# Transposing the queries and keys of the later chunks on the DMA crossbar instead of TensorE

## The chip, the cores and the metric

The kernel runs on one core of one Trainium2 chip. The metric is the device time of one execution in microseconds; a kernel's time is the median of its runs. A profiled execution has its own span, 1.7 to 2.0 us shorter than the time of the same run.

## The reference

A retention layer (attention with a decay in place of the softmax) over 8 batches, 8 heads, 576 positions and head size 64 makes a matrix of 4608 rows by 512, and a two-layer network with a swish gate runs on those rows:

```python
scores = scale * np.matmul(q, k.transpose(0, 1, 3, 2))
gamma = 1.0 - 2.0 ** (-5.0 - np.arange(H, dtype=np.float32))
Dmat = np.where(rel >= 0, gamma[:, None, None] ** rel[None, :, :], 0.0)
attn = np.matmul(scores * Dmat[None], v)
x = attn.transpose(0, 2, 1, 3).reshape(B * S, H * D)      # 4608 x 512
h = x @ w_in                                             # 512 -> 2048
g = h * (1.0 / (1.0 + np.exp(-beta * h)))
out = g @ w_out                                          # 2048 -> 512
```

## The kernel before

The retention part works in 40 chunks, five a batch: four of 128 positions and one of 64. For each chunk GpSimd casts queries, keys and values to bf16 (`pre`), TensorE transposes queries and keys in eight 128x128 blocks into PSUM and ScalarE copies them to SBUF (`a_T`), TensorE makes the scores (`a_sc`), the running state (`a_st`) and the output (`a_O`). The network works in nine blocks of 512 rows, each with 16 up steps and 16 down steps of four matmuls. The steps of the chunks for the next block are woven between the steps of the present block, at positions counted in fill steps (one fill step is one up or down step, four matmuls); the order in which they are called is the order in each engine's list.

```python
    def pre(i):
        # ...
        qn = sb.tile([P, H, D], BF16, name="qn", tag="qn", bufs=3)
        kn = sb.tile([P, H, D], BF16, name="kn", tag="kn", bufs=3)
        vp = vpads[i % NV]                    # NV = 3 padded value tiles, used in turn
        # ... casts: queries, keys, values (GpSimd from chunk 4 on)

    def a_T(i):
        # ...
        T = psum.tile([P, 2, HP, P], BF16, name="T", tag="T", bufs=1)
        for j, src in enumerate((L["qn"], L["kn"])):
            for p in range(HP):
                nc.tensor.transpose(T[:, j, p, :cL],
                                    src[:cL, 2 * p:2 * p + 2, :].rearrange("p h d -> p (h d)"),
                                    ident[:cL, :cL])
        qkT = sb.tile([P, 2, HP, P], BF16, name="qkT", tag="qkT", bufs=3)
        nc.scalar.copy(qkT[:, :, :, :cL], T[:, :, :, :cL])

    def up(m, fo, t0=0, tn=MB):
        # ...
        ph = psum.tile([P, MB], F32, name="ph", tag="mm", bufs=3)
        for ko in range(KO):
            nc.tensor.matmul(ph[:, :tn], w_in_sb[:, ko, fo * P:(fo + 1) * P], xT[:, ko, x0:x0 + tn], ...)
        nc.scalar.activation(gT[:, fo, t0:t0 + tn], ph[:, :tn], ACT.Silu, scale=beta_sb[:, fo:fo + 1])

    def attn_steps(i, at, gap=2.0):
        return [(at - 4, F(pre, i)), (at - 3.9, F(load_next, i)), (at, F(a_T, i)), (at + gap, F(a_sc, i)),
                (at + 2 * gap, F(a_st, i)), (at + 2 * gap, F(a_O, i))]
```

SyncE issues all loads and stores. Each load of a chunk is three DMAs (queries, keys, values) and runs seven chunks ahead.

## Time and profile before

| | before |
|---|---|
| time, median | 338.75 us (338.43 to 338.87) |
| TensorE busy | 97% of the span |
| ScalarE, VectorE, GpSimd busy | 48%, 34%, 34% |
| granted TensorE clock | 0.994 |

In a group of the profile, the columns are line, engine, operation, output<-inputs, count, then busy us and the mean of one in ns, then the idle time of the engine before them and what ended it. In a timeline they are start us, length us, engine, line, operation, count, and in brackets an idle time and what ended it. Matmul ends are modelled and overlap the next one, so a length in microseconds is read from start to start. The lines of the kernel before stand in the prediction below.

A ruler for what follows: the time from the first up step of block 2 to the first up step of block 8, read from the timeline. In these six blocks all 26 changed chunks are handled and TensorE is the bound. For the kernel before it is 305.50 - 95.89 = **209.61 us**.

### The profile page before, as it was taken

What the parts mean: (1) busy time and instruction counts of PE and PEld (TensorE: products, weight loads), DVE (VectorE), ACT (ScalarE), POOL (GpSimd) and SP (SyncE); (2) the same over time, 40 slices, a digit from 0 to 9 for tenths busy, and PEclk for the clock granted to TensorE, in tenths of its full rate; (3) what the DMA queues carried; (4) which work ended last, traced back from release to release, by engine and by line L of the source; (5) the groups of instructions that cost most, each with busy time, mean ns of one, the idle gap of its engine ahead of it and who ended that gap; (6) DMA issues with size and microseconds to landing.
All of it is one profiled execution on the core that took longest, in us unless ns stands there. A gap on an engine that the chain in (4) does not pass through costs nothing.

```text
span 337.1 us, 6009 instructions
## 1 busy us (share of the span) xinstructions
PE 325.6 (97%) x2455; PEld 174.0 (52%) x2455; DVE 114.0 (34%) x202; ACT 163.1 (48%) x272; POOL 115.0 (34%) x132
## 2 busy tenths in 40 slices
PE   5979899999999999999999999999999999999995
PEld 2644574676554555545555555545555555544442
DVE  4664373623321244213332432223224432320011
ACT  2767671385246623752376227712782257404800
POOL 5224767875324433323334432233333330000000
PEclk9799999999999999999999999999999999999999
DMA  9999999999999737906492549036400100011011
GB/s 173 222 387 212 243 377 214 199 212 229 234 222 246 146 111 172 172 0 158 116 228 48 117 118 214 9 87 159 114 2 31 61 36 0 14 55 57 2 61 63
DMA packets 121979, 46.53 MB, mean 138 GB/s; under 512 B 113232, under 2 KB 113248, under 8 KB 121952
## 3 DMA queue, kind: packets, MB, share of 16 engines
q1 hardware_dynamic: 121920, 46.15, 61.3%
q8 instruction: 19, 0.31, 0.4%
q14 instruction: 8, 0.07, 0.1%
q10 hardware_dynamic: 32, 0.01, 0.0%
HBM read 36.71 MB, written 9.44 MB: 137 GB/s over the span
## 4 chain that ended last, share of the span: by engine, by line
PE 84%; DMA 7%; SPq 4%; issue 1%; DVE 1%; ACT 1%; POOL 0%; POOLq 0%
PE po L285 38%; PE ph L273 32%; DMA qkvn<-in_q_dram 4%; PE O L238 4%; PE T L201 4%; SPq L63 4%; PE sc L217 3%; DMA wt<-in_moe_w_out_dram 2%; PE st L255 2%; PE O L233 2%; SPq L122 1%; ACT gT L275 1%; DVE w_out_sb L141 0%; DVE R L221 0%; ACT qkT L205 0%
## 5 line engine op out<-in xcount | busy, mean ns | idle before, releaser
L273 PE MATMUL ph<-xT,w_in_sb 128*128 128x512 bf16 (+2 forms) x640 | 134.2, 358 | 1.7 <-DVE xT L242 1.7
L285 PE MATMUL po<-w_out_sb,gT 128*128 128x512 bf16 x576 | 133.6, 380 | 0.0
L275 ACT ACTIVATE gT<-ph,beta_sb 128x512 bf16<-128x512 f32 (+2 forms) x160 | 102.0, 645 | 41.2 <-PE ph L273 39.9
L273 PEld LDWEIGHTS <-w_in_sb 128*128 128x128 bf16 x640 | 58.4, 98 | 55.5 <-issue 1.6
L285 PEld LDWEIGHTS <-gT 128*128 128x128 bf16 x576 | 53.3, 98 | 57.9
L221 DVE TENSOR_TENSOR R<-sc,causal 128x512 bf16<-128x512 f32 (+1 forms) x80 | 47.2, 631 | 101.1 <-PE sc L217 101.0
L205 ACT COPY qkT<-T 128x1024 bf16<-128x1024 bf16 (+1 forms) x40 | 36.9, 924 | 68.6 <-PE T L201 68.5
L181 POOL TENSOR_TENSOR qn<-qkvn,gq 128x512 bf16<-128x512 f32 (+1 forms) x36 | 37.9, 1052 | 49.9 <-PE T L201 46.4
L186 POOL TENSOR_TENSOR vpad<-qkvn,gv 128x512 bf16<-128x512 f32 (+1 forms) x40 | 41.6, 1041 | 28.2 <-PE O L238 14.9
L291 DVE COPY ot<-po 128x512 f32<-128x512 f32 x36 | 24.8, 691 | 67.5 <-PE po L285 65.1
L185 POOL CAST kn<-qkvn 128x512 bf16<-128x512 f32 (+1 forms) x36 | 21.9, 608 | 69.5 <-issue 65.7
L261 ACT CAST sbd<-st 64x256 bf16<-64x256 f32 x64 | 23.3, 364 | 43.4 <-PE st L255 42.6
L242 DVE CAST xT<-O 128x512 bf16<-128x512 f32 (+1 forms) x40 | 25.5, 637 | 38.0 <-PE O L238 38.0
L238 PE MATMUL O<-R,vpad 128*128 128x128 bf16 (+1 forms) x320 | 23.7, 214 | 1.4 <-DVE R L221 1.2
L238 PEld LDWEIGHTS <-vpad 128*128 128x128 bf16 (+1 forms) x320 | 18.2, 97 | 2.8 <-issue 2.2
L217 PEld LDWEIGHTS <-qkT 64*128 64x128 bf16 (+1 forms) x320 | 8.9, 98 | 17.3 <-ACT qkT L205 7.1
L201 PE MATMUL T<-ident,qn 128*128 128x128 bf16 (+1 forms) x160 | 15.1, 218 | 2.5 <-DVE qn L181 2.4
L201 PEld LDWEIGHTS <-qn 128*128 128x128 bf16 (+1 forms) x160 | 11.1, 99 | 11.9 <-DVE qn L181 2.4
L217 PE MATMUL sc<-qkT 64*128 64x128 bf16 (+1 forms) x320 | 15.5, 217 | 0.6 <-ACT qkT L205 0.4
L201 PE MATMUL T<-ident,kn 128*128 128x128 bf16 (+1 forms) x160 | 14.9, 216 | 0.3 <-POOL kn L185 0.3
L255 PEld LDWEIGHTS <-kn 128*128 128x128 bf16 x128 | 9.5, 99 | 6.6 <-issue 0.2
L255 PE MATMUL st<-vpad,kn 128*128 128x128 bf16 x128 | 12.7, 222 | 0.0
(40 smaller groups left out, 80.0 us busy)
## 6 DMA issues: line engine op xcount, KB each, us to landing
out_dram<-ot SPq DMA_DIRECT2D x36, 256.0 KB, 2.2
qkvn<-in_q_dram SPq DMA_DIRECT2D x32, 256.0 KB, 4.8
qkvn<-in_k_dram SPq DMA_DIRECT2D x32, 256.0 KB, 5.1
qkvn<-in_v_dram SPq DMA_DIRECT2D x32, 256.0 KB, 5.0
wt<-in_moe_w_in_dram SPq DMA_DIRECT2D x4, 1024.0 KB, 10.6
wt<-in_moe_w_out_dram SPq DMA_DIRECT2D x4, 1024.0 KB, 10.2
qkvn<-in_q_dram SPq DMA_DIRECT2D x8, 128.0 KB, 4.0
qkvn<-in_k_dram SPq DMA_DIRECT2D x8, 128.0 KB, 3.6
```

The lines of the kernel that those rows point to most:

```text
L181: (nc.vector if first else nc.gpsimd).tensor_tensor(qn[:cL], t[:cL, 0], gq_b, ALU.mult)
L186: nc.gpsimd.tensor_tensor(vp4[:cL], t[:cL, 2].rearrange("p (pr two) d -> p pr two d", two=2), gv_b.rearrange("p (pr two) d -> p pr two d", ...
L201: nc.tensor.transpose(T[:, j, p, :cL], src[:cL, 2 * p:2 * p + 2, :].rearrange("p h d -> p (h d)"), ident[:cL, :cL])
L205: nc.scalar.copy(qkT[:, :, :, :cL], T[:, :, :, :cL])
L217: nc.tensor.matmul(sc[j][:cL, p, :cL], L["kT"][r, p, :cL], L["qT"][r, p, :cL], start=True, stop=True, skip_group_check=True)
L221: nc.vector.tensor_tensor(R[:cL, j, :, :cL], sc[j][:cL, :, :cL], m_b, ALU.mult)
L238: nc.tensor.matmul(O[:, p, :cL], vp[:cL, 2 * p + j, :], R[:cL, j, p, :cL], start=(n == 0), stop=(j == 1), skip_group_check=True)
L242: nc.vector.tensor_copy(xT[:, :, n0:n0 + cL], O[:, :, :cL])
L255: nc.tensor.matmul(st[:, p, :], L["kn"][:cL, 2 * p:2 * p + 2, :].rearrange("p h d -> p (h d)"), L["vp4"][:cL, p], start=(c == 0 and p == 0 ...
L273: nc.tensor.matmul(ph[:, :tn], w_in_sb[:, ko, fo * P:(fo + 1) * P], xT[:, ko, x0:x0 + tn], start=(ko == 0), stop=(ko == KO - 1))
L275: nc.scalar.activation(gT[:, fo, t0:t0 + tn], ph[:, :tn], ACT.Silu, scale=beta_sb[:, fo:fo + 1])
L285: nc.tensor.matmul(po[:], gT[:, fo, ms * P:(ms + 1) * P], w_out_sb[:, fo, :], start=(fo == 0), stop=(fo == FO - 1))
```

## The change

Intent: take the transposes off TensorE, which is the bound, and give them to the DMA crossbar (the DMA engines' own transpose, issued with `dma_start_transpose`), for chunks from the last one of batch 2 on (chunk 14), where the loads are less dense. Queries and keys share one tile so that one DMA moves both; buffers grow from three to four; casts and transposes are placed earlier. The whole diff:

```diff
--- before.py
+++ after.py
@@ -64,6 +64,7 @@
         qkv_tiles[(b, c)] = t
 
     NQ = 7
+    XB = 14
     order = [(b, c) for b in range(B) for c in range(NC)]
     for b, c in order[:4]:
         load_chunk(b, c)
@@ -171,8 +172,8 @@
         c0, cL = chunks[c]
         t = qkv_tiles.pop((b, c))
         first = i < 4
-        qn = sb.tile([P, H, D], BF16, name="qn", tag="qn", bufs=3)
-        kn = sb.tile([P, H, D], BF16, name="kn", tag="kn", bufs=3)
+        qk = sb.tile([P, 2, H, D], BF16, name="qk", tag="qk", bufs=4)
+        qn, kn = qk[:, 0], qk[:, 1]
         vp = vpads[i % NV]
 
         vp4 = vp.rearrange("p (pr two) (x d) -> p pr (two x) d", two=2, x=2)[:, :, 0::3, :]
@@ -185,11 +186,21 @@
             nc.gpsimd.tensor_copy(kn[:cL], t[:cL, 1])
         nc.gpsimd.tensor_tensor(vp4[:cL], t[:cL, 2].rearrange("p (pr two) d -> p pr two d", two=2),
                                 gv_b.rearrange("p (pr two) d -> p pr two d", two=2), ALU.mult)
-        live[i] = dict(qn=qn, kn=kn, vp=vp, vp4=vp4)
+        live[i] = dict(qk=qk, qn=qn, kn=kn, vp=vp, vp4=vp4)
 
     def load_next(i):
         if i + NQ < len(order):
             load_chunk(*order[i + NQ])
+
+    def a_X(i):
+
+        b, c = order[i]
+        cL = chunks[c][1]
+        L = live[i]
+        qkT = sb.tile([P, 2, HP, P], BF16, name="qkT", tag="qkT", bufs=4)
+        nc.scalar.dma_start_transpose(qkT.rearrange("p j pr s -> p (j pr) s")[:, :, :cL],
+                                      L["qk"][:cL].rearrange("p j h d -> p (j h d)"))
+        L["qT"], L["kT"] = qkT[:, 0], qkT[:, 1]
 
     def a_T(i):
         b, c = order[i]
@@ -201,7 +212,7 @@
                 nc.tensor.transpose(T[:, j, p, :cL],
                                     src[:cL, 2 * p:2 * p + 2, :].rearrange("p h d -> p (h d)"),
                                     ident[:cL, :cL])
-        qkT = sb.tile([P, 2, HP, P], BF16, name="qkT", tag="qkT", bufs=3)
+        qkT = sb.tile([P, 2, HP, P], BF16, name="qkT", tag="qkT", bufs=4)
         nc.scalar.copy(qkT[:, :, :, :cL], T[:, :, :, :cL])
         L["qT"], L["kT"] = qkT[:, 0], qkT[:, 1]
 
@@ -308,7 +319,10 @@
 
     def attn_steps(i, at, gap=2.0):
 
-        return [(at - 4, F(pre, i)), (at - 3.9, F(load_next, i)), (at, F(a_T, i)), (at + gap, F(a_sc, i)),
+        if i < XB:
+            return [(at - 4, F(pre, i)), (at - 3.9, F(load_next, i)), (at, F(a_T, i)), (at + gap, F(a_sc, i)),
+                    (at + 2 * gap, F(a_st, i)), (at + 2 * gap, F(a_O, i))]
+        return [(at - 10, F(pre, i)), (at - 9.9, F(load_next, i)), (at - 5, F(a_X, i)), (at + gap, F(a_sc, i)),
                 (at + 2 * gap, F(a_st, i)), (at + 2 * gap, F(a_O, i))]
 
     warm_up(12)
```

## The prediction

> **What bounds the kernel now.** I read the busy table first, then the groups, then the chain of work that ended last, then the timeline of one block of rows. The busy table and two of the groups (columns of a group: line, engine, operation, output<-inputs, count | busy us, mean ns of one | idle us before it):
>
> ```profile
> PE 325.6 (97%) x2455; PEld 174.0 (52%) x2455; DVE 114.0 (34%) x202; ACT 163.1 (48%) x272; POOL 115.0 (34%) x132
> ...
> L205 ACT COPY qkT<-T 128x1024 bf16<-128x1024 bf16 (+1 forms) x40 | 36.9, 924 | 68.6 <-PE T L201 68.5
> ...
> L201 PE MATMUL T<-ident,qn 128*128 128x128 bf16 (+1 forms) x160 | 15.1, 218 | 2.5 <-DVE qn L181 2.4
> ...
> L201 PE MATMUL T<-ident,kn 128*128 128x128 bf16 (+1 forms) x160 | 14.9, 216 | 0.3 <-POOL kn L185 0.3
> ```
>
> TensorE is the bound; no other engine passes half of the span. The transposes look like 15.1 + 14.9 = 30 us, but a matmul's end is modelled and overlaps the next one's, so this sum must not be used as a saving. The timeline of TensorE (start us, length, engine, line, operation, count) gives start to start:
>
> ```profile
> 170.62 2.75 PE L273 MATMUL ph<-xT,w_in_sb 128*128 128x512 bf16 x12
> 173.21 0.39 PE L201 MATMUL T<-ident,qn 128*128 128x128 bf16 x4
> 173.43 0.39 PE L201 MATMUL T<-ident,kn 128*128 128x128 bf16 x4
> 173.65 1.89 PE L273 MATMUL ph<-xT,w_in_sb 128*128 128x512 bf16 x8
> 175.48 0.40 PE L217 MATMUL sc<-qkT 64*128 64x128 bf16 x8
> 175.81 1.90 PE L273 MATMUL ph<-xT,w_in_sb 128*128 128x512 bf16 x8
> 177.54 0.39 PE L255 MATMUL st<-vpad,kn 128*128 128x128 bf16 x4
> 177.77 0.39 PE L233 MATMUL O<-qkT,sbd 128*128 128x128 bf16 x4
> 177.99 0.61 PE L238 MATMUL O<-R,vpad 128*128 128x128 bf16 x8
> 178.44 1.89 PE L273 MATMUL ph<-xT,w_in_sb 128*128 128x512 bf16 x8
> 180.26 0.29 PE L201 MATMUL T<-ident,qn 64*128 64x64 bf16 x4
> 180.39 0.28 PE L201 MATMUL T<-ident,kn 64*128 64x64 bf16 x4
> 180.60 1.90 PE L273 MATMUL ph<-xT,w_in_sb 128*128 128x512 bf16 x8
> ```
>
> The reader is to see that TensorE never waits: 12 matmuls of 512 columns take 173.21 - 170.62 = 2.59 us (0.216 each), and everything else is packed against them. Eight transposes of a full chunk take 173.65 - 173.21 = 0.44 us, not 0.8. The 64-row chunk at 180.26 takes 0.34 us plus 0.09 us before it (178.44 + 8 x 0.216 = 180.17). In the window from 100 to 300 us the table by windows has TensorE at 100% of every stretch, granted clock 1.00. So each microsecond of work taken off TensorE there is a microsecond off the span, unless a wait appears.
>
> **What the Trainium skill says.** (1) "VectorE: DVE Perf Modes", section "The three transpose paths", puts a 128x128 bf16 transpose at 390 ns on TensorE and 1309 ns on the crossbar. The trace has 190 to 315 ns for one TensorE transpose and 0.44/8 = 55 ns in a row, so here the TensorE side is seven times cheaper than the page's figure; that caps what the change can win. (2) "Advanced Engine Details and Errata", section "X-Bar Transpose (TRN2)", says that such transposes run about as fast as regular DMAs. No run yet shows it. (3) "DMA: Bandwidth & Descriptors", section "Issuing engines are not separate DMA queues": DMAs of all issuers share 16 engines, and issuing from ScalarE only saves issue time. The trace agrees in so far as the loads, all from SyncE, already fill those engines: DMA share 0.61 from 130 to 170 us, 0.72 to 210, 0.36 to 250, then 0.09. (4) The same page, section "Queues, rings and completion order", gives older generations 262,144 sequencer cycles for 8,192 tiles of an SBUF to SBUF transpose, which is 32 a tile. No row of the trace shows such an issue.
>
> **The change part by part.** Chunks 14 to 39 change, 26 of 40; six of them (the last of batches 2 to 7) have 64 rows.
>
> *Removed from TensorE:* 20 full sets x 0.44 us = 8.8, and 6 short sets x 0.43 = 2.6, together **11.4 us**, all of it in the stretch where TensorE sets the end. The built program agrees: 208 transposes (26 x 8) are gone from its list. If nothing else happened: 338.75 - 11.4 = **327.3 us**.
>
> *Removed from ScalarE:* 20 copies of 1.01 us and 6 of 0.58 = 23.7 us. ScalarE is not the bound, so this is worth nothing by itself.
>
> *Added to ScalarE:* 26 DMA issues. The built program cuts the source into tiles of 16 rows by 128 columns: 8 x 8 = 64 for a full chunk. With 32 cycles a tile and the 1.2 GHz sequencer of "Advanced Engine Details and Errata" (Clock Domains), my estimate is 64 x 32 / 1.2 = 1.7 us of held ScalarE, half of that for a short chunk; the loads' own issues on SyncE took 0.38 to 2.87 us for the queries (median 0.77), so a full queue can stretch it. While ScalarE issues, it evicts no ph. Is that seen? The up-projection makes one ph per 4 x 0.216 = 0.863 us, ScalarE takes 0.69 us for each, and three buffers stand between. Taking the issue that falls at 168.0 us in the trace above: ScalarE is free at 168.45, holds to 170.15, evicts the two waiting tiles by 171.6; TensorE, which has scores, state and output of the earlier chunk to do meanwhile, asks for these buffers at 171.5 and 172.35, and the first was free by 170.9. So 1.7 us hides; past some 2.3 us the excess shows in TensorE. About half of the issues fall into up-projections, the rest into down-projections, where ScalarE has almost nothing to do. I charge 1 us in all.
>
> *Added to the DMA engines:* 26 transfers, 256 KB each for a full chunk. Loads of the same size (1024 packets of 256 bytes) land in 4.8 to 5.1 us in the median, three being issued together; the q1 queue spends 0.613 x 337 x 16 / 121,920 = 27 ns a packet, so 64 packets an engine are 1.7 us of work. Estimate for one transpose: 1.7 us of issue, overlapping 1.7 us of moving, doubled when a load shares the engines, and the 1 to 2 us of tail that the 2.2 us landing of the output stores suggests: 4 to 6 us.
>
> *Moved:* the transpose is issued 5 fill steps before the place of the old one, and scores follow 2 steps after that place. For the chunk transposed at 173.21, five steps before is 167.99 and its scores are at 175.48: 7.5 us, less the 0.44 us that goes, less the 0.45 us until ScalarE is free: 6.6 us. The data arrive in time by 0.6 to 2.6 us if the estimate holds. Inputs are ready: GpSimd's casts move six steps earlier, GpSimd is 34% busy and took 1.04 + 0.61 + 1.04 us a chunk, and the four buffers of queries and keys let it run ahead. I charge 2 us in all for transposes that land late, mainly before 210 us where loads fill the queues.
>
> *Sum:* 338.75 - 11.4 + 1 + 2 = 330.35, rounded to **330 us** (-2.6%).
>
> **The rivals.** *A: the score matmuls wait for late transposes.* For it: the new load of a chunk is issued about when a neighbour's transpose is, on the same engines, with landings up to 14.9 us for one load, and the skill's 1309 ns for one 128x128 block would make eight 10.5 us if they ran one after another. Against it: 6.6 us of lead, and a lead of five steps with four buffers looks chosen with care. If each came 1 us late, 26 us would come back and the time would be some 353 us; a wait in a third of them gives 336.
> *B: ScalarE becomes the bound of the up-projection.* An up-projection needs 16 x 0.72 us of eviction, about 2.5 x 0.74 of state copies and 2.5 issues: 13.4 us + 2.5 issues, against 16 x 0.863 + 2.5 x 1.33 = 17.1 us of TensorE. At 1.7 us an issue this is 17.6 against 17.1, just balanced by the buffers; at 3 us it is 20.9 and costs about 3 us in each of six blocks: some 345 us. Against it: the copy of 1 us that goes was in the same place without harm.
> *C: all is hidden,* and the change gives its full 11.4 us: 327.3.
> *D: the loads are pushed back by the transposes.* Against it: the last load is issued at 238 us for chunks used up to 300 us, seven chunks ahead; there is room.
>
> **Range and chances.** The floor is firm at 327.3, since only TensorE's sets are removed and nothing else on it changes; with trace error 326.5 is the low end. The high end, 341, takes in a partial A or B. Faster by over 2% means under 332.1, that is, losses under 4.8 us: 0.56. Between, up to 345.5: 0.32. Slower needs most transposes to be late or the issue to hold over 3 us: 0.12.
>
> **What would show it.** The transposes' line on TensorE should fall from 320 matmuls to 112, and start to start the neighbouring matmuls should close up by 0.44 us a chunk. In the table of DMA issues the transposes should land in 4 to 6 us, and their issue on ScalarE's queue should be 1.5 to 2 us. TensorE should stay above 96% busy. A is shown by waits of the score matmuls (or their weight loads) on the transpose DMA, longer before 210 us; B by waits of ph on the ScalarE eviction in the up-projections only. The prediction is wrong if either sum passes 5 us, or if TensorE's set cost less than 0.44 us in truth.

## The result

The changed kernel takes **327.03 us** (median of 4 runs, 326.51 to 328.84), against 338.59 us of the kernel before. A ratio here is the mean time of one kernel's runs over the mean of the other's runs of the same rounds, so it isn't quite the ratio of the medians: 0.9668, 95% interval 0.963 to 0.9706. It is 3.3% faster, clear of noise, and within the stated range. The granted clock is 0.992 against 0.994, so the clock is not the gain.

The busy table and the two groups of the page after (the transposes are now line 212, the copy line 216, the up matmuls line 284):

```profile
PE 311.7 (96%) x2208; PEld 163.8 (50%) x2247; DVE 114.4 (35%) x202; ACT 141.6 (44%) x246; POOL 113.3 (35%) x132
...
L216 ACT COPY qkT<-T 128x1024 bf16<-128x1024 bf16 (+1 forms) x14 | 13.3, 950 | 21.8 <-PE T L212 21.7
...
L212 PE MATMUL T<-ident,qk 128*128 128x128 bf16 (+1 forms) x112 | 8.7, 224 | 3.1 <-DVE qk L182 3.0
```

The transposes fell from 320 matmuls to 112, the copies from 40 to 14, and TensorE is still 96% busy: it is still the bound, with less to do. (Its own count, 2208 against 2247 weight loads, lacks some records.)

The timeline of the changed kernel in the block that the prediction showed:

```profile
163.90 0.69 ACT L286 ACTIVATE gT<-ph,beta_sb 128x512 bf16<-128x512 f32 x1 [0.17 <-PE ph L284]
163.98 1.25 ACTq L201 DMA_TRANSPOSE qkT<-qk  x1
...
165.28 1.47 ACT L286 ACTIVATE gT<-ph,beta_sb 128x512 bf16<-128x512 f32 x2 [0.69 <-PE ph L284]
...
166.75 4.48 PE L284 MATMUL ph<-xT,w_in_sb 128*128 128x512 bf16 x19
...
170.49 1.21 ACTq L201 DMA_TRANSPOSE qkT<-qk  x1
...
171.17 0.40 PE L228 MATMUL sc<-qkT 64*128 64x128 bf16 x8
...
171.75 0.69 ACT L286 ACTIVATE gT<-ph,beta_sb 128x512 bf16<-128x512 f32 x1 [0.65 <-PE sc L228]
```

Where a row of transposes cut the up matmuls, 20 of them now stand in a row: 171.17 - 166.75 = 4.42 us, of which 20 x 0.216 are 4.32 (one record is missing, hence x19). The issue occupies ScalarE's queue for 1.25 us and starts while ScalarE is still evicting a tile. It does hold ScalarE: here, and after each of the 15 issues whose next ScalarE instruction is the eviction of an up step, this eviction starts 0.05 us after the issue has ended (165.23 and 165.28; 171.70 and 171.75), although the view names TensorE. From the last weight load of a tile to its eviction it is 0.63 us where no issue stands between; after these 15 it is 0.69 to 1.16 us, 1.11 for the eviction at 171.75. So an eviction comes up to 0.53 us late, and the experiments below show that TensorE does not feel it.

How the transposes fared, in the view of their line (issue time min/median/max in ns; landing in us), and the one place where TensorE waited for one, in its timeline:

```profile
L201 ACTq DMA_TRANSPOSE qkT<-qk x26: 1210/1249/1561, 97.6 to 278.3; - x26
...
  PE sc L228: 0.4, 1
...
DMA to landing us min/median/max: 2.6/3.2/7.1
```

```profile
140.67 1.27 ACTq L201 DMA_TRANSPOSE qkT<-qk  x1
...
147.54 0.23 PEld L228 LDWEIGHTS <-qkT 64*128 64x128 bf16 x8 [0.88 <-DMA qkT<-qk]
147.54 0.40 PE L228 MATMUL sc<-qkT 64*128 64x128 bf16 x8 [0.39 <-DMA qkT<-qk]
```

The reader is to see that in the profiled run 25 of 26 transposes cost TensorE no wait. One, issued at 140.67 and landed 6.8 us later, cost 0.39 us.

The ruler gives the whole account:

| block | before | after | difference | chunks changed |
|---|---|---|---|---|
| 2 | 35.86 | 33.63 | 2.23 | 5 |
| 3 | 34.08 | 32.76 | 1.32 | 4 |
| 4 | 35.86 | 33.63 | 2.23 | 5 |
| 5 | 34.09 | 32.30 | 1.79 | 4 |
| 6 | 35.86 | 33.63 | 2.23 | 5 |
| 7 | 33.86 | 32.53 | 1.33 | 3 |
| sum | 209.61 | 198.48 | 11.13 | 26 |

Five blocks give 0.443 to 0.448 us a chunk changed (whose transposes fall in that block). Block 3, with the one late transpose, gives 0.46 us less than its four chunks should (4 x 0.445 = 1.78). So 26 x 0.445 = 11.57, less 0.46, is 11.11; the ruler has 11.13.

### The profile page after: what moved, and what is told of

The parts are those of the page before. It is cut to its first block, busy times and chain, and to the rows that moved or that the text cites.

```text
span 325.5 us, 5518 instructions
## 1 busy us (share of the span) xinstructions
PE 311.7 (96%) x2208; PEld 163.8 (50%) x2247; DVE 114.4 (35%) x202; ACT 141.6 (44%) x246; POOL 113.3 (35%) x132
## 3 DMA queue, kind: packets, MB, share of 16 engines
q1 hardware_dynamic: 121920, 46.15, 63.8%
q10 hardware_dynamic: 24416, 6.04, 11.3%
## 4 chain that ended last, share of the span: by engine, by line
PE 91%; DVE 3%; DMA 2%; ACT 1%; issue 1%; ACTq 0%
PE po L296 38%; PE ph L284 37%; PE O L249 5%; PE sc L228 4%; PE st L266 2%; DMA qkT<-qk 2%; PE ph L152 2%; PE O L244 2%; PE T L212 2%; DVE R L232 1%; ACT qkT L216 1%; ACT sbd L272 0%; DVE xT L253 0%; DVE w_in_sb L130 0%; DVE tiny L160 0%
## 5 line engine op out<-in xcount | busy, mean ns | idle before, releaser
L284 PE MATMUL ph<-xT,w_in_sb 128*128 128x512 bf16 (+2 forms) x623 | 131.4, 357 | 2.5 <-DVE xT L253 1.6
L296 PE MATMUL po<-w_out_sb,gT 128*128 128x512 bf16 x556 | 130.2, 379 | 1.1 <-issue 0.2
L182 POOL TENSOR_TENSOR qk<-qkvn,gq 128x512 bf16<-128x512 f32 (+1 forms) x36 | 37.8, 1051 | 2.1 <-DMA qkvn<-in_q_dram 1.6
L216 ACT COPY qkT<-T 128x1024 bf16<-128x1024 bf16 (+1 forms) x14 | 13.3, 950 | 21.8 <-PE T L212 21.7
L186 POOL CAST qk<-qkvn 128x512 bf16<-128x512 f32 (+1 forms) x36 | 21.9, 608 | 1.1 <-DMA qkvn<-in_k_dram 1.1
L228 PEld LDWEIGHTS <-qkT 64*128 64x128 bf16 (+1 forms) x320 | 8.9, 98 | 17.7 <-issue 11.4
L266 PEld LDWEIGHTS <-qk 128*128 128x128 bf16 x128 | 9.5, 99 | 6.6 <-issue 0.2
L266 PE MATMUL st<-vpad,qk 128*128 128x128 bf16 x128 | 12.6, 222 | 0.1
L212 PE MATMUL T<-ident,qk 128*128 128x128 bf16 (+1 forms) x112 | 8.7, 224 | 3.1 <-DVE qk L182 3.0
L244 PE MATMUL O<-qkT,sbd 128*128 128x128 bf16 (+1 forms) x128 | 11.5, 212 | 0.0
L212 PEld LDWEIGHTS <-qk 128*128 128x128 bf16 (+1 forms) x112 | 7.2, 103 | 5.1 <-DVE qk L182 3.1
```

What stands on the lines that cost most here:

```text
L182: (nc.vector if first else nc.gpsimd).tensor_tensor(qn[:cL], t[:cL, 0], gq_b, ALU.mult)
L228: nc.tensor.matmul(sc[j][:cL, p, :cL], L["kT"][r, p, :cL], L["qT"][r, p, :cL], start=True, stop=True, skip_group_check=True)
L266: nc.tensor.matmul(st[:, p, :], L["kn"][:cL, 2 * p:2 * p + 2, :].rearrange("p h d -> p (h d)"), L["vp4"][:cL, p], start=(c == 0 and p == 0 ...
L296: nc.tensor.matmul(po[:], gT[:, fo, ms * P:(ms + 1) * P], w_out_sb[:, fo, :], start=(fo == 0), stop=(fo == FO - 1))
```

## The experiments

Twelve kernels ran, in three sessions; the kernel before ran beside each and took 338.75, 338.67 and 338.87 us in the median. "Ruler" is the six-block time of the profiled run, which leaves out the varying start.

| run | what | time us | ratio to before (95%) | ruler us |
|---|---|---|---|---|
| before | | 338.6 to 338.9 | | 209.61 |
| after | the change | 327.03 | 0.9668 (0.963 to 0.9706) | 198.48 |
| e1_all_tensor | tiles and buffers only | 339.43 | 1.0014 (1.0 to 1.0027) | 209.61 |
| e2_pe_sets_back | TensorE's sets added again | 338.55 | 0.9999 (0.9978 to 1.002) | 209.60 |
| e3_act_copy_back | ScalarE's copies added again | 327.84 | 0.968 (0.9661 to 0.9698) | 198.02 |
| e4_no_transpose | nobody transposes (wrong result) | 327.62 | 0.9681 (0.966 to 0.9702) | 197.99 |
| e5_lead_one | lead of 1 step | 349.30 | 1.0304 (1.0244 to 1.0363) | 218.90 |
| e6_lead_three | lead of 3 steps | 336.33 | 0.9929 (0.9901 to 0.9958) | 206.89 |
| e8_from_sync | issued by SyncE | 330.37 | 0.9742 (0.9705 to 0.9779) | 201.84 |
| e9_from_27 | chunks 27 to 39 only | 334.17 | 0.9857 (0.9822 to 0.9891) | 203.81 |
| e10_from_32_lead_three | chunks 32 to 39, lead of 3 | 336.22 | 0.9906 (0.9879 to 0.9934) | 206.04 |
| e11_from_32_more_loads | the same beside more loads | 338.57 | 0.9986 (0.9969 to 1.0004) | 209.20 |
| e7_from_9 | chunks 9 to 39 | 333.89 | 0.9846 (0.9807 to 0.9885) | 198.87 |
| e12_from_9_lead_eight | chunks 9 to 39, lead of 8 | 336.64, wrong result | 0.9931 (0.9904 to 0.9959) | 198.03 |

### What is the gain made of?

A set is the eight transposes of one chunk. My theory was that TensorE's removed sets are all of the gain. The rivals: the larger buffers and the fused tile; the relief of ScalarE, which loses 23.7 us of copies.

**e1_all_tensor**, all transposes on TensorE, everything else as in the change:

```diff
-    XB = 14
+    XB = 40
```

> The fused query-key tile and the larger buffer counts of the change, but every transpose on TensorE. If the gain is TensorE's removed sets alone: the time of before, 338.6 us within 0.7. If the buffers or the layout carry part of it: below 337.

Measured 339.43 us, 0.8 over the 338.6 expected and so just outside the 0.7; the ruler is 209.61 as before to the hundredth. In the profiled run the whole excess lies ahead of the ruler, which begins at 97.38 us instead of 95.89. Tiles and buffers are worth nothing.

**e2_pe_sets_back**, the change with TensorE's sets at their old places, into a PSUM tile that nobody reads (`a_T0` is `a_T` without the copy):

```diff
-        return [..., (at - 5, F(a_X, i)), (at + gap, F(a_sc, i)),
+        return [..., (at - 5, F(a_X, i)), (at, F(a_T0, i)), (at + gap, F(a_sc, i)),
```

> The crossbar transposes stay, and TensorE again does its 26 sets of eight at the old places, with a result that nobody reads and no ScalarE copy. If TensorE's time is the gain: 327.0 + 26 x 0.44 = 338.5 us, within 1. If the relief of ScalarE (23.7 us of copies gone) is the gain: 327 to 329.

Measured 338.55 us, ruler 209.60: the whole gain is gone although the crossbar still delivers every transpose and ScalarE still has no copies for these chunks (busy for 141.6 us in both). Its timeline shows the set back between the matmuls, 175.29 - 174.84 = 0.45 us start to start:

```profile
172.25 2.75 PE L294 MATMUL ph<-xT,w_in_sb 128*128 128x512 bf16 x12
174.84 0.61 PE L225 MATMUL T<-ident,qk 128*128 128x128 bf16 x8
175.29 1.03 PE L294 MATMUL ph<-xT,w_in_sb 128*128 128x512 bf16 x4
```

**e3_act_copy_back**, the change with a ScalarE copy at each old place, 26 of 1.04 us (27.0 us, against the 23.7 us removed):

```diff
+    def a_C(i):
+        L = live[i]
+        dmy = sb.tile([P, 2, H, D], BF16, name="dmy", tag="dmy", bufs=1)
+        nc.scalar.copy(dmy[:chunks[order[i][1]][1]], L["qk"][:chunks[order[i][1]][1]])
 # ...
-        return [..., (at - 5, F(a_X, i)), (at + gap, F(a_sc, i)),
+        return [..., (at - 5, F(a_X, i)), (at, F(a_C, i)), (at + gap, F(a_sc, i)),
```

> The crossbar transposes stay, and ScalarE copies 128x1024 bf16 (some 1 us) at each old place into a tile that nobody reads. If TensorE's time is the gain: 327 us, at most 328.5. If ScalarE's relief is the gain: near 338. If ScalarE is now close to the bound of the up-projections, with issue and copy together 2.25 us a chunk: 329 to 333.

Measured 327.84 us, ruler 198.02. ScalarE carries issue and copy together without harm to TensorE (none of its 26 transposes was late at the scores), so its relief gave nothing, and the rival that it would become the bound falls too.

**e4_no_transpose**, from chunk 14 on the scores read a constant tile. Its output is wrong, which doesn't matter for the time.

```diff
+    fixT = consts.tile([P, 2, HP, P], BF16, name="fixT")
+    nc.gpsimd.memset(fixT[:], 0.01)
 # ...
-        qkT = sb.tile([P, 2, HP, P], BF16, name="qkT", tag="qkT", bufs=4)
-        nc.scalar.dma_start_transpose(...)
+        qkT = fixT
```

> Wrong result on purpose: from chunk 14 on the scores and the state product read one constant tile, and nothing is transposed by anyone. This is the floor of any way that takes the sets off TensorE. If the transfers are hidden: 326.0 to 327.0 us, that is, 0 to 1 us under the changed kernel. If they cost something (late arrivals, held ScalarE, loads pushed back): more than 1 us under it.

Measured 327.62 us, ratio 0.9681 against 0.9668 of the change: the same. On the ruler it has 197.99, the change 198.48. All that crossbar, issue and late arrival cost together is 0.5 us. The change sits on its floor.

**e9_from_27**, half the dose (`XB = 27`, 13 chunks):

> Only chunks 27 to 39 go through the crossbar, 13 of 26. If each set is worth 0.44 us: 338.7 - 13 x 0.44 = 333.0 us. If the gain sits in the early stretch, where loads are dense: above 335; if in the late one: below 331.

Measured 334.17 us where 333.0 was expected. The ruler is exact: 209.61 - 203.81 = 5.80 = 13 x 0.446. The rest of the difference lies in the start and the tail. Each chunk is worth the same, early or late.

### Why do the transposes come in time?

**e5_lead_one** and **e6_lead_three** place the transpose later, so that its lead (the fill steps from its issue to the old place of the set) is 1 or 3 instead of 5; the casts stay:

```diff
-        return [..., (at - 5, F(a_X, i)), ...
+        return [..., (at - 1, F(a_X, i)), ...      # e5; at - 3 in e6
```

> The transpose is placed 1 fill step before the old place instead of 5, so that 3 steps lie before its scores: 2.6 us of fill and up to 1.8 us of a neighbour's work, less some 0.4 us until ScalarE is free. Landing takes 3.2 us in the median and 7.1 at most. If lead hides the transfer: up to 1 us late each in the up-projections, where ScalarE keeps step with TensorE, none in the down-projections, where ScalarE runs ahead: 329 to 338 us with waits of scores on the transpose DMA. If the lead does not matter (ScalarE's list lets it run ahead anyway): 327 to 328.

> The transpose is placed 3 fill steps ahead: some 5.2 us before the scores, less 0.4. Landing of 3.2 us in the median fits with 1.5 us to spare; the slow ones (7 us) do not: 327 to 329 us.

Measured 349.30 and 336.33 us: both misses. The lead matters far more than I had said. The waits of TensorE in the two, e5 first (waiting group, releaser: total us, times, longest):

```profile
PE sc L228 <- DMA qkT<-qk: 18.1, 16, 2.3
```

```profile
PE sc L228 <- DMA qkT<-qk: 8.4, 7, 2.4
```

They account for most of the excess over the changed kernel (9.3 us in e6, 22.3 in e5; 8.0 and 20.4 for the profiled runs). In e5 TensorE also ran at a granted clock of 0.50 from 191.0 to 194.5 us; more on this under e8. My error was to reckon with the median landing of the whole span, 3.2 us. Landing depends on the stretch. Asked by windows, the changed kernel's transposes landed in 4.0 us (median) from 90 to 140 us, 4.6 (up to 7.1) from 140 to 180, 3.2 from 180 to 230, and 3.1 (2.6 to 3.3) after 230. Three rows of its table by windows (engines' busy time, then clock, DMA share, GB/s) show what else differs (the DMA share adds up the times of packets, so it can pass 1):

```profile
130.00:170.00 40.00, 39.34 (x265) 19.70 (x268) 11.88 (x20) 18.28 (x31) 12.97 (x15) 1.00 1.06 208
...
210.00:250.00 40.00, 39.68 (x265) 19.78 (x269) 12.39 (x20) 16.19 (x28) 14.50 (x17) 1.00 0.44 99
250.00:288.00 38.00, 37.74 (x256) 18.98 (x260) 12.51 (x21) 13.70 (x24) 6.22 (x7) 1.00 0.19 54
```

The slow stretch is the one where the DMA engines are full. That's a coincidence in time until it is tried, so:

**e10_from_32_lead_three** uses the short lead only for the last eight chunks, after the loads have ended; **e11_from_32_more_loads** is the same with seven chunks loaded again, which nobody reads:

```diff
-    XB = 14
+    XB = 32
-        return [..., (at - 5, F(a_X, i)), ...
+        return [..., (at - 3, F(a_X, i)), ...
         # e11 only:
-        if i + NQ < len(order):
-            load_chunk(*order[i + NQ])
+        load_chunk(*order[(i + NQ) % len(order)])
```

> Only the last eight chunks go through the crossbar, with the short lead of 3 steps; by then (from some 230 us) the loads of the changed kernel have ended and the DMA engines are busy for 0.2 to 0.4 of the time. If the loads on the same engines make transposes late: none is late here, landing stays near 3 us, and the time is 338.7 - 8 x 0.44 = 335.2 us. If the short lead alone does it: each is late by about the 0.35 us that the lead-three kernel lost per transpose, and the time is near 338.

> The same, with seven more chunks loaded again at the end (5.5 MB that nobody reads, into buffers that are free), so that loads run on beside these eight transposes. If competition with loads makes them late: landing goes up to 4 to 7 us, scores wait for the transpose DMA, and the time rises by 1 to 5 us over the run without the loads. If not: the same time as that run.

Measured 336.22 us for e10: ruler 206.04, 3.57 less than before, which is 8 x 0.446, and no wait of TensorE for a transpose. The total is 1 us over the expected 335.2; in the profiled run 0.6 us of it lie in the start (96.50 against 95.89). With the loads beside them, 338.57 us: the ruler goes up by 3.16 to 209.20. The rows by windows of e10, then of e11, and each one's landing:

```profile
230.00:260.00 30.00, 30.00 (x220) 15.48 (x215) 10.72 (x17) 14.62 (x25) 10.37 (x12) 1.00 0.49 100
```

```profile
DMA to landing us min/median/max: 2.7/3.1/4.0
```

```profile
230.00:260.00 30.00, 28.96 (x210) 14.92 (x208) 9.47 (x15) 14.62 (x26) 10.37 (x12) 1.00 1.02 179
```

```profile
DMA to landing us min/median/max: 2.7/4.4/6.1
```

```profile
254.07 0.40 PE L227 MATMUL sc<-qkT 64*128 64x128 bf16 x8 [1.04 <-DMA qkT<-qk]
...
284.10 0.40 PE L227 MATMUL sc<-qkT 64*128 64x128 bf16 x8 [1.78 <-DMA qkT<-qk]
```

Nothing but the loads differs, and they bring late transposes back: DMA share from 0.49 to 1.02, landing from 3.1 to 4.4 us in the median, 2.8 us of waits at the scores. That loads running beside the transposes lengthen their landing is shown; that a lead of five steps is what hides it follows from e6 against the changed kernel. Where the two meet (the engines, their order of service, the memory ports) was not tried.

**e8_from_sync** issues the same transposes from SyncE:

```diff
-        nc.scalar.dma_start_transpose(...)
+        nc.sync.dma_start_transpose(...)
```

> The same transposes, issued from SyncE, whose list also holds the loads (0.4 to 2.9 us each to issue) and the output stores, each of which waits for TensorE and VectorE. If who issues matters only by what stands ahead in its list: some transposes come late behind loads and stores, 329 to 335 us. If issuers do not matter: 327 to 328.

Measured 330.37 us, by the ratios 2.5 slower than the change. The ruler puts it all in block 2, 37.45 us against 33.63. SyncE's list there, and below it TensorE's:

```profile
99.36 0.86 SPq L63 DMA_DIRECT2D qkvn<-in_q_dram  x1
100.27 1.08 SPq L63 DMA_DIRECT2D qkvn<-in_k_dram  x1
101.40 0.98 SPq L63 DMA_DIRECT2D qkvn<-in_v_dram  x1
102.47 1.23 SPq L304 DMA_DIRECT2D out_dram<-ot  x1
103.81 1.33 SPq L201 DMA_TRANSPOSE qkT<-qk  x1
```

```profile
107.23 0.31 PE L228 MATMUL sc<-qkT 64*64 64x64 bf16 x8 [2.19 <-DMA qkT<-qk]
```

The first transpose stood behind loads and a store and was issued at 103.81, where ScalarE had issued it at 97.57 in the change; the scores waited 2.19 us. The other 1.6 us of the block are no wait but the clock, as its table by windows shows (the third number from the end is the granted clock):

```profile
109.00:112.00 3.00, 3.00 (x19) 1.45 (x18) 0.42 (x1) 0.93 (x2) 1.08 (x2) 0.50 1.29 217
112.00:115.00 3.00, 3.00 (x18) 1.28 (x18) 0.00 (x0) 2.07 (x4) 1.51 (x2) 1.00 1.32 223
```

From 108.5 to 112.0 us TensorE was granted a clock of 0.50, and its matmuls of 512 columns there start 0.427 us apart instead of 0.216: some 1.7 us lost on top of the wait. What makes the clock fall was not tried. After 60 us it fell three times in runs with a right result, each time beside a wait of TensorE: of 2.19 us here, 2.33 in e5 and 4.36 in e7. Waits of 2.36 us in e6 and of 2.35 and 2.24 in e5 brought no such stretch. Once the list was past this place, SyncE served as well as ScalarE: the later blocks are at the floor.

### Can more chunks go?

**e7_from_9** (`XB = 9`):

> Five more chunks, 9 to 13, go through the crossbar, lead 5 as in the change, in the stretch where loads are densest. Hidden, they save 5 x 0.44 = 2.2 us: 324.9. Late as under dense loads: 325 to 329.

Measured 333.89 us: neither. The ruler reads 198.87, 0.4 over the change and 0.9 over e4, with one wait of 0.80 us for a transpose. Chunks 9 to 13 lie ahead of the ruler, and so does the loss: the first up step of block 1 starts at 72.80 us instead of 66.52. The timeline there:

```profile
62.73 1.04 POOL L182 TENSOR_TENSOR qk<-qkvn,gq 128x512 bf16<-128x512 f32 x1
...
63.82 1.16 PE L212 MATMUL T<-ident,qk 128*128 128x128 bf16 x8 [4.36 <-POOL qk L182]
```

In this kernel the casts of chunk 9 are placed 10 steps before its slot, which puts them ahead of chunk 8's, whose casts are only 4 steps ahead. Chunk 9's first cast began at 59.44 us, after 2.79 us of waiting for its own load; chunk 8's only at 62.73. So TensorE, which still transposes chunk 8 itself, stood for 4.36 us. Then it ran at half the clock:

```profile
64.00:69.00 5.00, 5.00 (x25) 2.09 (x24) 0.73 (x2) 1.01 (x1) 5.00 (x7) 0.50 1.16 180
```

Eight matmuls of 512 columns, from 64.77 to 68.32 us, took 3.55 us there instead of 1.73. Further on, at 80.83, one chunk's scores waited 1.54 us for a transpose under dense loads (landing took 5.8 to 7.2 us before 100 us). The moved casts cost more than the late transposes.

**e12_from_9_lead_eight** (casts at 13 steps, transposes at 8):

> Chunks from 9 on, the lead raised from 5 to 8 steps and the casts from 10 to 13. With 3 more steps (2.6 us) even a landing of 7 us is in time: 338.7 - 31 x 0.445 = 324.9 us with no wait of the scores for a transpose. If more lead only moves the transposes onto other loads: like the run from chunk 9 with lead 5.

The result was wrong (relative error 0.21), and the fault is mine. There are three padded value tiles, and the built program has chunk 10's cast into one of them ahead of the matmuls that read chunk 7's values from it: by the positions in the code, 39.5 - 13 = 26.5 against 23 + 4 = 27; in the trace the cast is at 70.14 and those matmuls at 72.03 us. Dependencies keep the order of the list; they cannot repair it. So its time, and above all that of the early part, decides nothing. In the six blocks, where the order is sound, the ruler is 198.03 with landings up to 7.3 us and no wait for a transpose, so a longer lead does remove the last 0.45 us. A version that goes below the change (the casts of the early chunks left where they were) was not run, so the changed kernel remains the fastest here.

## Why the prediction was right

- **TensorE is the bound and a set is worth 0.44 us, not 0.8.** Right: 0.445 a chunk on the ruler, and e2 and e9 give it back in doses. Reading start to start instead of summing busy time was what set the size; the busy sums would have promised nearly twice as much.
- **The floor, 327.3 us.** Right: 327.03 measured, 327.62 with no transposes at all. Rival C, which was this floor, is what came; the 330 of the sum was not.
- **Nothing from ScalarE's relief.** Right (e3).
- **The issue: 1.7 us, half for a short chunk.** Too large for a full chunk and wrong in shape: 1.21 to 1.56 us whatever the size; the 64-row chunk 14 took 1.29. (The row of the page with 32 cycles a tile stands in the section "Why a DMA increments its semaphore by 16 and not by 1"; the section that the prediction named was wrong.) ScalarE is held, as the prediction said, and TensorE does not feel it: the charge of 1 us was 0 (e3 and e4). That the three buffers are the reason, as it reckoned, fits but was not tried.
- **Landing: 4 to 6 us.** 3.2 us in the median, 4.0 to 4.6 where loads are dense; the range holds for that stretch only. The charge of 2 us for late ones was 0.4, one wait. These two charges are 2.6 of the 3.3 us by which 330.35 missed; 0.2 more is that 26 x 0.445 is 11.6, not 11.4.
- **Crossbar packets cost about as much as ordinary ones.** Right, as "Advanced Engine Details and Errata", "X-Bar Transpose (TRN2)", of the Trainium skill says: 0.113 x 325.5 x 16 / 24,416 = 24 ns a packet in their queue (11.3% of 16 engines' span), 0.638 x 325.5 x 16 / 121,920 = 27 ns in that of the loads and stores. The second mean mixes sizes; by size in the same trace, packets of 256 bytes took 24.7 ns in the mean on the crossbar's queue and 22.4 on the other, 18 in the median on both.
- **The lead, 6.6 us.** Nearly right: the very chunk of that sum was issued at 163.98 and wanted at 171.17, 7.2 us, since the issue did not wait for ScalarE to be free; the late one was issued at 140.67 and wanted at 147.54 - 0.39, 6.5 us.
- **Rival A (late transposes)** is the real danger, and the lead is what keeps it off: e6 has lost most of the gain and e5 more than all of it. **Rival B (ScalarE)** is not seen on TensorE. **Rival C (all hidden)** is what happened. **Rival D (loads pushed back)**: no cost is seen on TensorE's side, and e4 without transposes is no faster.

## What to carry to other kernels

When an engine is the bound without gaps, the worth of taking an instruction off it is its spacing start to start there, and putting the same work back with its result unread (e2) proves the account. A transfer that takes over such work is free only as long as its lead covers its landing in the most loaded stretch, not the median over the span; the list of the issuing engine, and the lists of the engines whose work moves earlier with it, decide as much as the transfer itself. And a wait of TensorE can cost more than its length: in e8 a wait of 2.19 us was followed by 1.6 us more lost at half the clock.

## What the Trainium skill lacked or had wrong

- "VectorE: DVE Perf Modes", "The three transpose paths", gives 390 ns for a 128x128 bf16 transpose on TensorE. In a row they took 55 ns each here (0.44 us for eight), 190 to 315 ns from start to end of one, so the table makes a row of transposes on TensorE look dearer than it is.
- The same table gives 1309 ns for the crossbar without saying what several blocks in one DMA take: eight blocks landed in 3.1 to 3.3 us on quiet DMA engines, not 8 x 1.3.
- "DMA: Bandwidth & Descriptors", "Why a DMA increments its semaphore by 16 and not by 1", gives for older generations a count of cycles from which one expects an issue that grows with the number of tiles. Here, in the changed kernel, the issue took 1.21 to 1.56 us from ScalarE for full and for half chunks alike; no page has this.
- No page says by how much a crossbar transpose slows beside ordinary loads: 3.1 us in the median at a DMA share of 0.2 to 0.5 (e10), 4.4 us and up to 6.1 with only loads added (e11), 4.6 and up to 7.1 in the dense stretch of the changed kernel.
